# A new order for the first two fifths of a fused attention and gated-convolution kernel

## The chip, the core and the metric

The kernel runs on one core of one Trainium2 chip. A core has five engines that each work through a stream of their own: TensorE (PE in the profile, with its weight loads as PEld), VectorE (DVE), ScalarE (ACT), GpSimd (POOL) and SyncE (SP). They wait for one another through semaphores. Sixteen DMA engines move data between the memory outside the core and its on-chip memory, or within the latter. The metric is the device time of one execution in microseconds (us); lower is better.

## The reference

The inputs are q, k and v of 4 batches, 8 heads, 768 positions and 64 features, a table of sampled blocks, and the weights of a feed-forward stage. First comes block-sparse attention with blocks of 32 positions:

```
scores = scale * q @ k.T
mask   = |block_i - block_j| <= 1, or either block is the first or the last,
         or block_j is one of three sampled for block_i
attn   = softmax(where(mask, scores, -1e9)) @ v
```

The heads of a position are put side by side (512 features) and go through a gated convolution:

```
h    = relu(x @ w_in)                     # 512 -> 1024
conv = sum over k of conv_w[k] * h shifted by k - 1 along the sequence
out  = (h * sigmoid(conv)) @ w_out        # 1024 -> 512
```

## The kernel before, in words

**Tiling.** Two heads of one batch make a pair; there are 16 pairs, numbered P = 0 to 15, four to a batch. The 768 positions are taken in two halves of 384, so the run has eight segments of batch and half (the last is split once more). Scores are computed transposed, 128 keys by 128 queries at a time: eight such blocks fill one 128x1024 buffer `st` of PSUM (the memory that TensorE writes), and this is a unit, u = 0 to 143. A pair takes 4.5 units in each half; pair 0 comes at u = 0 and again at u = 18, pair 4 at u = 36 and u = 54, pair 5 at u = 40.5, pair 8 at u = 72.

**What happens to a unit.** TensorE computes two half units of scores (`s`, line 754) with the keys as weights; 24 more rows of the operands carry the mask, so the mask is added by the same matmul. ScalarE takes the exponential of the whole unit (`exp`, line 765) into a `pt` buffer. TensorE then multiplies by the values with a column of ones beside them (`av`, line 787). There are two `st` buffers, so the scores of a unit wait for the exponential two units back. When a pair is through, VectorE divides by the sums (`rcp`, line 703, and `norm`, line 705).

**Keys and queries.** They are needed transposed. For pairs 0 to 4, TensorE transposes them (`k_tr`, line 476, `q_tr`, line 515) and a copy puts them into the pair's slot (`k_cp`, `q_cp`, line 327, the helper that records all copies). For pairs 5 to 15 the transpose is done in a DMA issued by SyncE, a crossbar turn (`xb`, line 593, one for k and one for q), into a staging buffer, and two copies (`stg_cp`, line 327) put it into the slot. There are five slots. The mask rows of slots 1 and 2 are copied by VectorE; those of slots 3 and 4 by two DMAs of 144 KB on SyncE (`m_dma`, line 368). Pair 4 uses slot 4. Values go through one copy for each pair (`v_cp`, line 327).

**Feed-forward stage.** The normalised result of each pair and half has to be transposed too: with TensorE for the first segment (`x_tr`, line 724), and for later ones with another crossbar turn on SyncE (`x_xb`, line 714, into `xT`). When the four pairs of a segment are there, TensorE multiplies by `w_in` (`f1`, line 906, eight feature groups for a segment, in two entries each), VectorE or ScalarE applies the relu (`relu`, line 928 on VectorE, 926 on ScalarE), VectorE does the convolution (`mul`, line 967, `add`, line 976), ScalarE a tanh (line 1015), VectorE the gate (`g1`, line 1018, `g2`, line 1023). The second product (`f2`, line 833) waits for the gate of the feature groups that it reads; its four entries for an output block take two feature groups each. A copy (`ev`, line 327) and a DMA (`out`, line 841) end it.

**Loads.** GpSimd issues all loads of q, k, v and of the two weight matrices (line 240). Between them stand `pace` entries: a copy of a single element that reads a tile, so that GpSimd waits until that tile has landed (line 668) or until the exponential of a certain unit is done (line 425).

**What sets the order.** Each piece of work is an entry of a list (`op`). An entry has one or two engines that can do it, the buffers it takes, and guessed costs. A planner worked out an order from the costs before the kernel was written down; only its result is in the file, in the string `ORDER`. `put_down` reads it: two characters give the entry's number, a letter the engine where there is a choice (P, A, V, G, S), and a digit for each buffer that the entry takes. The kernel then issues the entries in that order, and every engine works through its own in turn:

```
o = ops[64 * CODE.index(line[x]) + CODE.index(line[x + 1])]
...
    e = ENGINES[line[x]]
...
for b in o.allocs:
    b.index = CODE.index(line[x])
...
    o.fn(e)
```

Semaphores follow from what each entry reads and writes. An engine never goes past an entry that waits: what stands behind it in its stream waits too.

Of the kernel before, what the change touches and what calls it, by code (L numbers as in the profile page):

```python
# [25 lines left out]
53415j5B60Q5k5E11RV35F5o18V5p5t5G71mV5J05K0L5u15C4I15L01nV5O15P4JV05D0H5405H5Q15X055V5Y5v25I0B5M5w5N5Z25R5S601
421M15T3615U5x15+06236505yV665V0435/0R5WV674630I1z16a1441S46b1BVhk01AV6c56f06g451T64hl6h668hn1hmV046220ho6n1hpV
6o6s0ht06p747hI02416t69hJ6dhC16u048hDhL256x1hK6yhEA6e49hu2a1hM6z16C0hq1hvV4ahr2c0hN6DhsVhw04bhx2d6E2hQ16K16L23V4
hz1hR6M34chA2i26P0hT6Q6ihyA6j1hO4d6q2k26U1hBV6R46V1N0hS1U14e2l6r6W5hU6Z06+1OV6/61PV7211VV473hF06k0747hGhY26v7a0
h+7bhV6w6l6A6B6F6GhHV6N06m17c0hW1X06H16Oi437f11ZA6S6ThP02601WA7g7k0hZ6X6Y7l7h1hX70ii127h/717m26I7p17q1YV756J7r3  # L30
i07x0ic0i5761i17y772id782e17C17z4i77d7e7Di27ii67j2f7n7E57o7H0i87I7s7ti37A0i97B7F797M17u37G7vij7J628V07Nik7w29V
7O7ie7Kia7R07Sib2m27L7P7Q2bV02jA17Z17+7T02gV1if2niligV07/18202s4f832q3imV17Uio0842ip7W04g1+02hV87188iqAir17X2t3
is8938c0itV8d2v2u7V1iA08e4iM48k1808liNiBiO8m58p08qiPix1iy8r62rV28u1iQ812w08586iCV8aiR8v8bizV8z08A8w72oV2iu07Y2
iv2pV8f8g8B08n08E1iwV8F2x1/18h18oiS8G18s8M0iU02D2E48NiD0iW8O2iE2A8i2B08t8R120V8SiFA8xiV8W02G8T32F8y8C8D21V8XiJ0
j018Y5j18/190iKiX914970j2988HiY8I18P9968Q8U8J2j39c18ViG1iLViZ9d8Z8K9h09i9e7iTiH8L8+j492939j0i+943i/8jiIAjm09a0
9m19n959r02O9o12P1j82jy196jzj92Lj59sja9z19bjb9f9t29g2H19kjnjc9l9Aj6jd9p2R9q2M2j79u2I9E09F9B39v1jejA2Qjfjo9G49J1
9KjB9L5jp2WjCV22X19C9O0jqA39P9w02yV39W19D9Q69X9xjH1jI9y39Y7jE0jF9/0a0jGA1jJV0E2S2a412Z2+0jK1a10k039Ha5k1jN0a61
jLk22TjOjMVa90aajPAk3ae1302/afab2k84ihjT1jUk49Iag39M0JjQ09N9Rka9Sam0jVA9T29Z00Fan35k53639+a2jR2zVa3ao4ar1asjSV
jZ1j+kg0at5aw0khaxjW0310k9ay6a7jrjX2JV4aB1a8aCkbjYAacadahaD79UaJ0aKkcjg0aL0jh2KVaO1aPaj1j/VjiaQ1k6aT0ko1aUjjak
kdai1apaqkpaY1alaZaV22CV3js12NV4aukjavaza+3aAinaEk71aFb10b2ki32jtjkA4kkb91b34bakrju9VaG3jvkebb52YV038be0392aH  # L40
kC0klaM0kqbfaIaNaRkfaSbg6bj1aWkmbkksaXa/kDjwA02UV03dbo03abl7bp2VVjxb0kw13bknb4ktb51kx3cbw1bq0bxkukykvkEby1b60
33V13jbB0kz37A1bCkAV3bG1bHkFbD2b7kI1kGV1b80kJbI3bcbL034VbMkL0bN4kKVkM3e1bQ1kNVbdbRbhbil42bm3mbS53k0kR13fbY0l5
bZ3n3bnl6kO0b+6c11l7jDc2kSl8c37kP3rkTVbr3obsc60c7bt1kQAbz0bu3pbAcb1c80cclc3bE3qkX1ldbFl9kYlecj0cklfcd1kU0kZVbJ
bKbObPlgbTcl2bU1co1bV2b/lal11bWcplhkVlbbXct0kWAc0c4lic5cq3c9calk4cuk+0ljbvk/cv4lll2celmcy1cfl0A3s2czln3AcD03x
cE3B4cA5cg3cm0l3Vcncrcscwlo3tlG0cF6ls0cL1lA1ltlpcxcMch3FcQ03CcBlvcRcN7cicClH3DlucGcH1cS1lBlwkBcOlqcPcV1lxlrcW
kHc+0c/3gV2cT3icX0lClyjlcUlzlId02d613hVd7cYlJd83lDlKV03G0db0lEA2dc3uV3dg13O3P1dhdd4lY0lZ3y2cZdi5m81l+V0m93EcI0
dl0cJd1dm3Tl/0maV3Qdn6m03vVdq13Rd2drm1Vd90m51ds73L3M1dy0mk1dzm20ml3SdA0m33Hmmm63ZdD1mn3+3dEm7AdadI0m4AmolLdJdF2
mb1d323lV23U1me0d4mfdK1ms2mcdemgVdN1dOmdAdfmtdjdkdP3dodpmA3dV0dWmCdtmh0dX4mBd+1d/du1mDcK1dBdCe05mimEe30d5e4mu
lM1mjAdv1dGe563VmvdHdLe81dwdMe9dQmpmwdRlNmI4dY0ea7dZlS0dS3mqlOmr0mFed0mJeelTmxmKlUdTlPef0mLe1lVmGe2mMel1lWA3em
3zV3e6eq0myen2e7ebmzermW0mHlQA1ecev13IV43KlFdxdUlX3wewmNegmXmQ1es1mOmRmPeh1ex3mS3JVmTei0eA0ejmUA4eBmY3WV0ek2mZ  # L50
# [5 lines left out]
oJgjgFoNgJ1gkoB1ouAoOoCgG1oU1gKgo1oy0oVgpgL3gtoWgugyozoXgR0oDAgSoPgzoAAgZ1gA3gH0oKgT4oa1gBgIgMoQobgO0g+p03oRgC0
h20p1h3gDAgN1ocoSg/5p2odoL1pk0oeA1p3plgPhb1p4pmAgUgQ0pt1oYh46gVh00pupw2o40gW2pvAgXh1pyh5gYo5p5pxo6pzoZo7h71p6
mVpn1p7o8A0poo+hcoTppApq0h8prhd7o/h61pE4pe1pFpsApfpApgpHh90phpU0haAhepVhfpiA2p80hg3hhp9pBpGpjpapXhi1pIpbhjApM3
qf1pcA4pNqgpCqhAqi0pdpOpJqjpPqc1ofqt0qkApDquqdpQqv1nZqy1qzpKqeAql0qwpRpLqmo9qo0qxqpqnApWq01qq2q1qA4qrpYq60qspZ
qD0pSqEq7pTqF1qBqI0p+qGp/q8qHq2qCq3q9q4A2qJqaA4qKq5qLqbqO1qMA1qPqQqRqNSqU0qSA3qVqWqXqTSqYAqZA  # L60
"""


# [1022 lines left out]
```

## Time and profile before

| | |
|---|---|
| median of 3 runs | 206.25 us (206.09 to 206.26) |
| profiled execution | 205.76 us, of which the span of instructions is 204.0 us |
| TensorE busy | 197.6 us (97%), 2408 matmuls |
| ScalarE busy | 190.0 us (93%) |
| VectorE busy | 182.5 us (89%) |
| GpSimd busy | 57.5 us |
| DMA traffic | 25.93 MB, 53341 packets |

The profile gives one execution. A busy time is a sum over instructions and takes in the time from an instruction's start to its end; instructions of one engine overlap by some hundredths of a microsecond, so the distance between the starts of two neighbours (called the pitch below) is what an instruction costs its engine. In the tables of stretches, each engine has its busy time and, in brackets, the number of its instructions; the DMA share is the mean over 16 engines and can come out over 1 since packets overlap. In a timeline, a row is a start, a length, and a merged run of like instructions; SPq and POOLq are the issuing of DMAs, whose data land later.

The median is 0.49 us over the profiled execution; the profiled execution is 1.76 us over its span.

### The profile page before, as it was taken

The page shows a single profiled execution, that of the slowest core. Times are in us where ns is not written, and L with a number is a line of the kernel's source. Part 1 is how long each engine was busy: PE and PEld are TensorE (multiplying, and loading weights), DVE is VectorE, ACT ScalarE, POOL GpSimd, SP SyncE. Part 2 cuts the span into 40 slices and gives each one's busy share as a digit, 9 for nine tenths or more (in the row PEclk, how much of TensorE's full clock was granted, in tenths as well). Part 3 has the DMA queues.
Part 4 walks back from the last instruction along what each step waited for, and adds up shares of the span by engine and source line. Part 5 has one row for each costly group of instructions (what it writes and reads, how often), then busy time and mean ns, then how long its engine had stood idle before and what let it go on. Part 6 is the DMA issues. An engine that isn't in the chain of part 4 may idle for free.

```text
span 204.0 us, 6214 instructions
## 1 busy us (share of the span) xinstructions
PE 197.6 (97%) x2408; PEld 143.3 (70%) x2408; DVE 182.5 (89%) x572; ACT 190.0 (93%) x251; POOL 57.5 (28%) x112
## 2 busy tenths in 40 slices
...
GB/s 137 163 207 204 197 138 133 149 150 137 94 157 106 139 126 184 191 121 130 148 80 172 96 138 239 140 155 170 78 112 23 39 16 64 16 10 59 190 70 206
DMA packets 53341, 25.93 MB, mean 127 GB/s; under 512 B 39352, under 2 KB 50320, under 8 KB 53312
## 3 DMA queue, kind: packets, MB, share of 16 engines
...
HBM read 23.08 MB, written 6.29 MB: 144 GB/s over the span
## 4 chain that ended last, share of the span: by engine, by line
PE 72%; DVE 9%; ACT 8%; DMA 4%; issue 3%; POOL 3%; ACTq 0%
PE st L754 22%; PE mix L833 18%; PE mix L906 16%; PE av L787 13%; ACT pt L765 7%; DMA nat<-in_q_dram 4%; DVE m L967 3%; DVE m L976 2%; DVE hE L928 1%; POOL nat L240 1%; PE mix L818 1%; PE st L833 1%; DVE qk L327 1%; DVE xtok L705 1%; POOL vn L240 1%
## 5 line engine op out<-in xcount | busy, mean ns | idle before, releaser
L765 ACT ACTIVATE pt<-st 128x1024 bf16<-128x1024 f32 x144 | 140.6, 1041 | 2.4 <-PE st L754 2.0
L754 PE MATMUL st<-qk 88*128 88x256 bf16 (+2 forms) x600 | 89.7, 267 | 1.3 <-ACT pt L765 1.1
L787 PEld LDWEIGHTS <-pt 128*128 128x128 bf16 x1152 | 53.7, 97 | 14.0 <-ACT pt L765 0.5
L754 PEld LDWEIGHTS <-qk 88*128 88x128 bf16 x600 | 48.5, 97 | 19.8 <-issue 2.0
L787 PE MATMUL av<-vt,pt 128*128 128x65 bf16 x1152 | 60.0, 193 | 0.1
L906 PE MATMUL mix<-xT,winb 128*128 128x384 bf16 (+2 forms) x288 | 54.0, 307 | 0.1
L967 DVE TENSOR_SCALAR m<-hE,cw 128x382 bf16<-128x382 bf16 (+2 forms) x192 | 49.7, 320 | 0.5 <-ACT hE L926 0.2
L833 PE MATMUL mix<-woutb,gT 128*128 128x512 bf16 x176 | 47.0, 379 | 0.3 <-DVE gT L1023 0.2
L976 DVE TENSOR_TENSOR m<-m 128x764 bf16<-128x764 bf16 (+2 forms) x64 | 33.7, 534 | 0.5
L906 PEld LDWEIGHTS <-winb 128*128 128x128 bf16 x288 | 24.3, 97 | 9.1 <-issue 0.5
L1015 ACT ACTIVATE m<-m 128x764 bf16<-128x764 bf16 (+2 forms) x32 | 26.4, 831 | 0.9 <-DVE m L976 0.8
L833 PEld LDWEIGHTS <-gT 128*128 128x128 bf16 x184 | 15.5, 97 | 10.7 <-DVE gT L1023 0.5
L425 POOL COPY pace<-pt 1x1 bf16<-1x1 bf16 x24 | 6.0, 250 | 53.0 <-ACT pt L765 52.9
L928 DVE TENSOR_SCALAR hE<-mix 128x384 bf16<-128x384 f32 x31 | 16.9, 552 | 3.2 <-PE mix L906 3.0
L705 DVE TENSOR_TENSOR xtok<-av,rcp 128x384 bf16<-128x384 f32 (+2 forms) x36 | 18.3, 507 | 0.4
L1023 DVE TENSOR_TENSOR gT<-m,hE 128x764 bf16<-128x764 bf16 (+3 forms) x36 | 18.1, 512 | 0.5
L240 POOL DMA_DIRECT2D nat<-in_q_dram x23 | 17.4, 758 | 2.5 <-issue 2.3
L926 ACT ACTIVATE hE<-mix 128x384 bf16<-128x384 f32 (+2 forms) x33 | 16.4, 509 | 0.7 <-PE mix L906 0.5
L327 DVE COPY qk<-stg 64x1536 bf16<-64x1536 bf16 x22 | 12.2, 555 | 0.4
L1018 DVE TENSOR_SCALAR m<-m 128x764 bf16<-128x764 bf16 (+3 forms) x36 | 11.8, 335 | 0.7 <-ACT m L1015 0.4
L240 POOL DMA_DIRECT2D vn<-in_v_dram x16 | 11.6, 727 | 2.5 <-issue 1.6
L327 ACT COPY o2s<-mix 128x512 f32<-128x512 f32 (+1 forms) x16 | 8.9, 564 | 3.5 <-PE mix L833 2.5
...
## 6 DMA issues: line engine op xcount, KB each, us to landing
...
vn<-in_v_dram POOLq DMA_DIRECT2D x16, 192.0 KB, 4.6
nat<-in_k_dram POOLq DMA_DIRECT2D x15, 192.0 KB, 4.6
nat<-in_q_dram POOLq DMA_DIRECT2D x7, 192.0 KB, 5.7
...
```

The lines of the kernel that those rows point to most:

```text
L240: return op(name, {eng: occ}, lambda e: on(e).dma_start(out=dst(), in_=src), prio, deps, dma=(kind, service), **kw)
L327: return (nc.scalar.copy if e == "ACT" else nc.vector.tensor_copy)(out=dst, in_=src)
L705: nm = op("norm", {"DVE": t_dps(128 * C)}, lambda e: nc.vector.tensor_tensor(out=xtok_t[xk.index][:, 0:C].rearrange("p c h d -> p h c d"), ...
L754: nc.tensor.matmul(out=st[:, 128 * x:128 * (x + n_)], lhsT=QK_t[s][0:88, 1, hh, kc, :], rhs=QK_t[s][0:88, 0, hh, at:at + n_, :].rearrange( ...
L765: nc.scalar.activation(out=pt_t[ptb.index], in_=st_t[stb.index], func=AF.Exp, bias=0.0, scale=0.125)
L787: nc.tensor.matmul(out=o[:, off:off + 65], lhsT=pt_t[ptb.index][:, 128 * x:128 * x + 128], rhs=V_t[vslot_b[P].index][:, hh, kc, 0:65], sta ...
L833: nc.tensor.matmul(out=acc(), lhsT=gT_t[gb.index][:, ffc, 128 * t:128 * t + 128], rhs=woutb[:, ffc, :], start=(ffc == 0), stop=(ffc == NFF ...
L906: nc.tensor.matmul(out=mix_t[hb.index][:, w1 * y:w1 * y + w1], lhsT=winb[:, fc, 128 * ffc:128 * ffc + 128], rhs=xT_t[xt_buf[n].index][:, f ...
L928: i = nc.vector.tensor_scalar(out=dst, in0=src, scalar1=0.5, scalar2=0.0, op0=ALU.mult, op1=ALU.max)
L967: i = nc.vector.tensor_scalar(out=m_t[cb.index][:, x, y, 0:w], in0=hE_t[heb.index][:, f0 + y, t0 + x:t0 + x + w], scalar1=cw[:, x, f0 + y: ...
L976: nc.vector.tensor_tensor(out=m[:, a_, :, 0:w], in0=m[:, a_, :, 0:w], in1=m[:, b_, :, 0:w], op=ALU.add)
L1015: th = [op("tanh", {"ACT": t_act(2 * w) + 0.04}, lambda e, cb=cb, w=w: nc.scalar.activation(out=m_t[cb.index][:, 0, :, 0:w], in_=m_t[cb.in ...
```

## The change

Only the string `ORDER` differs. The entries are the same 1783; no instruction is added or taken away. Read entry by entry, the streams of the engines are the same as before from some point to the end: the last 507 of 894 entries on TensorE (from `f1` 39, the second entry of the fourth feature group of the third segment, which before starts at 80.48 us), 157 on ScalarE, 270 on VectorE, 58 of 85 on SyncE, and 35 of 108 on GpSimd. In front of that they are arranged anew. Some buffers get other numbers throughout.

```diff
 ORDER = """
-0405000v010x020bq+107060z03q/r01c0r10w0er208r3r4r5r60c090ar7r81dr9ra0gVrbrcrdrerf1a00hArg0drhrirjrkrl0UA10nV1o1
-rmrnro0frp0SArqrr0W01q20oA0y1010irsrt0XA0rurv160rwrxry12ArzrA0VV0TArB1k1rCrDrE11A130rF0jV0mArG1r4h00YV4i15A0Z1
...
+0405000x0w01020b070603rH0q+1q/1c00yr00cr108r2r3r4r40er5091dr6r7r80dr9rarbrc0ard1a0re0gV0hArfrgrhrirj0nVrk0UA11o1
...
 """
```

Decoded, these are the parts that matter for what follows (a number is the entry's place among entries of its name, counted from 0).

| stream | before | after |
|---|---|---|
| SyncE, after the start | m_dma slot 3, m_dma slot 4, x_xb 0, xb 0, xb 1, x_xb 1, xb 2, xb 3, x_xb 2, x_xb 3, xb 4, xb 5 | m_dma slot 3, x_xb 0, m_dma slot 4, xb 0, xb 1, xb 2, xb 3, xb 4, xb 5, x_xb 1, x_xb 2, x_xb 3 |
| SyncE, then | xb 6, x_xb 4, xb 7, x_xb 6, x_xb 5, x_xb 7, xb 8, xb 9, x_xb 8, xb 10, xb 11, out | xb 6, x_xb 4, xb 8, x_xb 6, x_xb 5, x_xb 7, xb 9, xb 7, xb 10, xb 11, x_xb 8, out |
| GpSimd, after the first five loads | second half of q of pairs 0 and 1, then q of 2, v of 2, k of 3, q of 3 | q of 2, v of 2, k of 3, q of 3, then second half of q of pairs 0 and 1 |
| GpSimd, later | v of pair 10 and q of pair 10 before the pace on u = 63 | both behind the pace on u = 63 |
| VectorE, first half of batch 0 | relu 3, relu 2, mul, v_cp of pair 4 | v_cp of pair 4, relu 2, mul |
| VectorE, at the staging copies | norm 7, stg_cp 0, stg_cp 1 | stg_cp 0, g1, two add, rcp, g2, stg_cp 1, norm 7 |
| TensorE, around the first `f1` of the second segment | s 84, s 85, av, f1 16, f1 17, s 86, s 87, f1 18, f1 19 | s 84, s 85, f2, s 86, s 87, f1 16 to 19 |
| TensorE, the 12 dummy matmuls `fill` | between u = 2 and u = 4 | one at the very start, one at the first transposes, ten spread up to u = 11 |

Twenty-eight entries change between VectorE and ScalarE: six `relu` each way; `stg_cp` 5, an `ev`, an `x_cp`, a `q_cp`, two `k_cp` and a `cast_k` from VectorE to ScalarE; a `v_cp`, an `ev`, three `q_cp`, two `k_cp`, `m_h1` and `m_kh` from ScalarE to VectorE. VectorE ends up with two entries more and ScalarE with two fewer.

More of the change, by code (lines that the diff above doesn't have):

```diff
@@ L26 @@
[L26 to L50, printed above, removed]
@@ L56 @@
[L56 to L60, printed above, removed]
+0405000x0w01020b070603rH0q+1q/1c00yr00cr108r2r3r40er5091dr6r7r80dr9rarbrc0ard1a0re0gV0hArfrgrhrirj0nVrk0UA11o1
@@ new lines @@
+rlrm0frnro0SArp0W01q2rq0VArI0i101rrrsrtru1r0Z1rvrw0XV012A11Arx0/Aryrz0+V1C2rArB0YA4h00lV4i0mV1E30TArC0oVrD0jV
+rErF4j00prG0t4m11F1314n1e115V14V4o11601h00z1fV14r04s1k11jV4t24w11iV4x1Q30v0q4y34B01gV4C4D41bV04K11pV14L0M4k14l
+0s4p4M54q4P00N4Q0rrJ1s04R64U11tV20O4V1v14W71xV4Z04+0P1wV4u4v4z1uV4/0rK5614A570k400C1rLrMrNrO581rP5b00D5c0G1G0
+1J15d20I5g15h1HV34ErQrRrS4F05i31KV4N5l04G05m1LV4O4S1IV4T5n44X5q15r1DV21l11RV34Y5s5504H5z05A511nV5915a5B65215e
+5E1535F5f1mV5j5k5G75o0A5p5J05K1705t5L05O119V1y05P0L5u05C5D5415Q118V415H0Q5I5v25X05w5Y5M425N1M15R5S6015T3615U4I0
@@ new lines @@
+434JV055A5Z25x16236500R665yV5V00B1z1674445WV1S46a11AV6bhk01BV6c5hl450H1T6f06ghmV0hn1466h6220ho6n1hpV6ohq06p76s0
+47hI02416tht1hJhu6u048hL6x1256yhK5+15/636z149642a1hrhM6C06D23V44ahvA682c0hsV696K16E26L6dhQ16e4bhz12dhShNhA1N0
+hR6P0hBA4c6Q2i2hT6i1PA6j0hw16M3hU6q6r4dhx2k2hO6v6k16R46whyV6U16V4e6A2lhY26B6F6W56Z06l6GhC14f1OV6m1hDhVhZ6+721
+h+1U06/6hEV730u6N16O6S1VV41X17477a0260hW7b6T1ZV6X6Y1WV7c0707f17gh/hF07h1hG6H06I717k0277lhP0hHA757607dhX7m27e7p1
+7q1YV2e17iii0i437r37ji07n2f7o7x0i57yi1ic17722m2i6id7z4787C17D28V0ij2n7E5i27H07Ii77s7t7A17J6i87M16J7B7F7u37Ni3
@@ new lines @@
+7Gi97K29Vie797O77L7v7R07Sikia7T0ib7w7Z17+2gV1il7/12bV08202s2q3imV083if8422t3871igV188io04g8931+0ip2hVir1iqVis
+2v2u8c0itV8d8k18l2oV22pAix08m4iM47Piu1iN7Q7U7V02w0iv8e5iPiyiwV8p18qizAiO8u02A8r62B08081iU08viA1iViB8w785iQ8z1
+868a7W18AiXiR8b8f8giCV8E08F8B08h0iJ0iS2jV1iD1iTiK8G18M12DiW2E48NiE8iiLA8R0iFV8O28n08o8SiY8s8t8xj018y8T38C8W12G
+2Fj18X1/08D8Y521V8/08H2rV2iG18J2iH7XiZ9020V8I17Y28P914iIV8Q97198j28U8V8Z996j32H19c09di+jm0i/9e79h19ij48+jn9j0
+j829m0ja929njy1j58K2O932P19r1j98L9a09o19b9f943j69s9gjb9k9ljz9t28jjc9p9z0j79q9Ajd9E195jo9B39F96je9ujAjf9v19G49C
@@ new lines @@
+9J02I9Kjp9L6jBjqV29O12x9PjCA39w19W09x9X9Q79DjE00E2S2jF9Y0jH1jGV1jI9/1a0jJAjK02Z2yV32La11a402M1a5k03jN12+0jLk1
+a639HjOk22Ra912QjMVaajPAae0k3afab52W30jT02X2k84jU9Ik4ag29M2/jQ10J9N9R9Sam1kajVA9Z0an35k53639T29+0Fa2jRa3ao42zV
+ar0as2TjZ0jSVj+at6aw1kg0axjW1kh9y3ay7a7jXk9aB02JV4a8aCjYAacihkbadahaD0aJ19UaKjg1kcaL1jh2KVaO0aPjiaj0j/VaQ3aT1
+310aUk6jrjjko1kdai1akapaqaY0kpaZaV5aljs02CV3au2NV4avaza+2kjaAaEaFinb11k71b2jtjkA4ki32b90b34bakkjukrjv9Vbb6aG3
+ke38be1392kC12YV0aHklaM0bfkqaNaIaRaSbg7bj0kfaWbkkmaXa/kDksjwA13dbo12UV03abl0bpjxb0kw02VV3bb4ktb51knkx3cbw0bq1
@@ new lines @@
+bxkukykvkEby3b6133V13jbB1kz37A1bCkAV2bG0bHkFbD5b7kI0kGV0b80kJbI2bcbL134VbMkL1bN4kKVkM3e1bQ0kNVbdbRbhbil42bm3m
+bS63k0kR03fbY1l5bZ3n4bnl6kO1b+7c10l7jDc2kSl8c30kP3rkTVbr3obsc61c7bt0kQAbz0bu3pbAcb0c81cclc3bE3qkX0ldbFl9kYlecj1
+cklfcd3kU1kZVbJbKbObPlgbTcl5bU1co0bV2b/lal10bWcplhkVlbbXct1kWAc0c4lic5cq2c9calk4cuk+1ljbvk/cv4lll2celmcy0cfl0A
+3s2czln3AcD13xcE3B3cA6cg3cm0l3Vcncrcscwlo3tlG1cF7ls0cL0lA0ltlpcxcMch3FcQ13CcBlvcRcN0cicClH3DlucGcH1cS3lBlwkBcO
+lqcPcV0lxlrcWkHc+1c/3gV2cT3icX1lClyjlcUlzlId05d603hVd7cYlJd82lDlKV1db1lEA3dc3uV3dg03O3P1dhdd4lY1lZ3G03y1cZdi6
@@ new lines @@
+m80l+V0m93EcI1dl1cJd1dm3Tl/1maV3Qdn7m03vVdq03Rd2drm1Vd90m50ds03L3M2dy1mk1dzm21ml3SdA1m3mmm63ZdD0mn3+3dEm7AdadI1
+m4AmodJdF5mb0d323lV2me1d4mfdK3ms2mc3HdemgVdN0dOmdAdfmtdjdkdP2lLdodpmA3dV1dWmC3U1dtmh1dX4mBd+0d/du1mDdBdCe06mi
+mEe31e4mulM0mjAdv0dGe57mvdHdLe80dwdMe9cK1dQmpmwdRlNmI4d5dY0ea0dZlS1dS3mqlO3Vmr0mFed1mJeelTmxmKlUdTlPef1mLe1lV
+mGe2mMel0lWA2em3zV3e6eq1myen5e7ebmzermW1mHlQA0ecev03IV43KlFdxdUewlXmNegmX3wmQ0es3mOmRmPeh1ex2mS3JVmTei1eA1ejmUA4
+eBmY3WV0ek2mZeI0m+V1eJn90lRna3XVn613Yn73NV43/A0eC4eK6m/eN1nbVn8AeOeS0eTeP7nw0n30nyn4n01eU0nxn1n5VeX1eYn2Anzeo
```

17 lines of the change are left out of this document (9 added, 8 removed).

## The prediction

> **What bounds the kernel now.** I read the page's shares and its chain first, then a table of stretches, then the timelines of the engines around the places that the new order touches.
>
> ```profile
> span 204.0 us, 6214 instructions
> PE 197.6 (97%) x2408; PEld 143.3 (70%) x2408; DVE 182.5 (89%) x572; ACT 190.0 (93%) x251; POOL 57.5 (28%) x112
> PE 72%; DVE 9%; ACT 8%; DMA 4%; issue 3%; POOL 3%; ACTq 0%
> ```
>
> ```profile
> 5.00:36.00 31.00, 30.22 (x418) 24.06 (x418) 27.14 (x85) 29.76 (x38) 18.71 (x36) 1.00 1.20 173
> 36.00:46.00 10.00, 9.04 (x131) 6.97 (x128) 9.89 (x32) 9.95 (x14) 3.39 (x7) 1.00 1.21 150
> 46.00:62.00 16.00, 16.00 (x212) 11.66 (x210) 15.08 (x41) 16.00 (x20) 4.32 (x10) 1.00 0.86 123
> 62.00:76.00 14.00, 13.68 (x171) 9.29 (x170) 12.75 (x38) 13.58 (x18) 5.40 (x12) 1.00 1.01 131
> 76.00:80.50 4.50, 4.50 (x45) 3.09 (x43) 3.79 (x13) 4.50 (x7) 1.82 (x3) 1.00 1.33 197
> 80.50:180.00 99.50, 99.50 (x1217) 70.53 (x1216) 93.82 (x282) 97.29 (x124) 19.82 (x36) 1.00 0.65 110
> ```
>
> TensorE's clock is 1.00 in every stretch. From 80.5 to 180 us TensorE has no idle time, and its stream there is the same before and after; so the change can act only through the moment at which TensorE reaches that point, which I call the handover: `f1` 39 at 80.48 us, inside this run:
>
> ```profile
> 74.25 0.56 DVE L1023 TENSOR_TENSOR gT<-m,hE 128x772 bf16<-128x772 bf16 x1
> 75.22 1.03 PE L833 MATMUL mix<-woutb,gT 128*128 128x512 bf16 x4
> 79.83 1.14 PE L906 MATMUL mix<-xT,winb 128*128 128x384 bf16 x6
> ```
>
> The work in front of the handover is the same matmuls. Only idle time can go or come: 0.78 us from 5 to 36, 0.96 from 36 to 46, 0.32 from 62 to 76, and 1.10 in the first 5 us. So no order gains more than about 3 us, and one that keeps the startup gains at most 2. In that front part ScalarE and VectorE are nearly full too (9.95 and 9.89 of 10 from 36 to 46): a stall of either comes out on TensorE.
>
> Nothing there waits for the crossbar. The staging tile's own view has one wait of 0.2 us:
>
> ```profile
> L593 SPq DMA_TRANSPOSE stg<-nat x22: 1209/1238/2119, 42.0 to 136.0; - x22
> PEld L754: 0.2, 1
> DMA to landing us min/median/max: 2.8/4.7/7.7
> ```
>
> **The change part by part.** I follow the new streams with pitches from this trace and note when the three engines pass four places.
>
> *Up to 33 us: the loads.* The second halves of q for pairs 0 and 1 go behind four loads, and so q of pair 2, for which TensorE stands 0.17 us at 14.26, leaves at 5.2 instead of 6.6.
>
> ```profile
> 6.60 0.77 POOL L240 DMA_DIRECT2D nat<-in_q_dram  x1
> 14.26 0.40 PE L515 MATMUL mix<-ident,nat 128*128 128x128 bf16 x4 [0.17 <-DMA nat<-in_q_dram]
> POOL pace L668 <- DMA woutb<-in_moe_w_out_dram: 3.5, 2, 2.3
> 28.72 0.71 POOL L240 DMA_DIRECT2D vn<-in_v_dram  x1
> vn<-in_v_dram POOLq DMA_DIRECT2D x1, 192.0 KB, 4.3
> 33.58 0.56 DVE L928 TENSOR_SCALAR hE<-mix 128x384 bf16<-128x384 f32 x1 [0.33 <-PE mix L906]
> 34.66 0.35 DVE L327 COPY vt<-vn 128x768 bf16<-128x768 bf16 x1
> ```
>
> That, the spread dummies and copies moved off ScalarE let the exponentials run up to 1.5 us earlier by u = 26. It is worth little, because of the next entry: VectorE now copies the values of pair 4 ahead of `relu` 2. They leave at 28.72 and need 4.3, so they are there at 33.0, and GpSimd's chain up to there hangs on the landing of weight loads (3.5 us of waits) that stay where they are. VectorE arrives at about 31.5 and stands; behind it wait `relu` 2, its PSUM buffer `mix`, and so the next transpose on TensorE. It goes on at 33.1, and `relu` 2 starts at 33.4: before, 33.58. The early gain is given back but for 0.2, and 0.27 of copying is done.
>
> *33 to 47.5 us: the first crossbar turns.*
>
> ```profile
> 40.09 0.54 DVE L705 TENSOR_TENSOR xtok<-av,rcp 128x384 bf16<-128x384 f32 x1
> 39.16 0.71 POOL L240 DMA_DIRECT2D nat<-in_k_dram  x1 [0.21 <-issue]
> 7.51 1.79 SPq L368 DMA_DIRECT2D qk<-qk  x2
> 40.65 1.28 SPq L714 DMA_TRANSPOSE xT<-xtok  x1
> 42.04 2.69 SPq L593 DMA_TRANSPOSE stg<-nat  x2
> xT<-xtok SPq DMA_TRANSPOSE x1, 5.3
> 45.00:47.00 2.00, 2.00 (x25) 1.33 (x24) 1.97 (x8) 2.00 (x3) 0.00 (x0) 1.00 1.27 219
> 47.00:47.50 0.50, 0.50 (x19) 0.50 (x18) 0.47 (x3) 0.50 (x2) 0.00 (x0) 1.00 0.23 38
> ```
>
> `norm` 4, ten VectorE pitches behind `relu` 2 (some 4.6 us), ends near 37.9 instead of 40.6, so SyncE starts 2.7 us sooner. But between its first turn and the next now stands the mask copy of slot 4, 144 KB, which before went out with its sister within 1.79 us from 7.51. It needs SyncE for half of that, 0.9, and the DMA engines at their busiest. The turn that went out at 40.65, behind loads still on their way, landed only after 5.3 us, when these were through; the DMA share is over 1 until 47 and 0.23 after it, so the turns issued by 44.8 were done then. The new burst holds the same loads and turns up to `xb` 1, plus the copy: at 219 GB/s its 144 KB are 0.67 us. Beside short rows such a copy takes partly idle bandwidth; bounds are 0 and 0.67, and I take the middle: `xb` 1 lands at 47.5 (47.1 to 47.8). VectorE comes to its first staging copy, 13.2 us of pitches behind the value copy, at 46.2: it stands 1.3 us. The mask itself is wanted by the scores of pair 4 at about 44.6. Issued at 39.3, between two loads, it should be there by 44.1; behind the load of 40.14 it would take till 46. TensorE has 1.3 us to spare before the next place, so even that costs at most 0.4.
>
> *47.5 us to `f1` 16.*
>
> ```profile
> 48.58 0.56 DVE L705 TENSOR_TENSOR xtok<-av,rcp 128x384 bf16<-128x384 f32 x1
> 49.06 1.13 DVE L327 COPY qk<-stg 64x1536 bf16<-64x1536 bf16 x2
> 49.68 2.51 SPq L714 DMA_TRANSPOSE xT<-xtok  x2
> 50.49 0.60 PE L754 MATMUL st<-qk 88*128 88x128 bf16 x4
> 53.16 0.81 PE L906 MATMUL mix<-xT,winb 128*128 128x384 bf16 x4
> L714 SPq DMA_TRANSPOSE xT<-xtok x29: 1107/1205/1721, 40.7 to 182.9; - x29
> DMA to landing us min/median/max: 2.3/2.7/5.3
> ```
>
> Between the two staging copies stand now `g1`, two `add`, `rcp` and `g2`; the second ends 2.9 us behind the first's start, at 50.5, about as before (50.2). The scores of pair 5, which stood at 50.71 (second half of the unit at 50.49), stand at 50.6. From there TensorE has 2.8 us up to `f1` 16, and 0.15 of waiting for the gate: 53.55. `norm` 7 ends at 51.0; the last turn that `f1` 16 needs leaves at 51.1 and at the shortest landing of its tile, 2.3 us, is there at 53.4. SyncE, with nine turns at 1.27 and the copy from 37.9, is free by 50.2. So `f1` 16 starts at F = 53.6, 0.44 later than before, with 0.07 more of TensorE's work done.
>
> *From `f1` 16 to the handover.*
>
> ```profile
> 55.10 0.56 DVE L928 TENSOR_SCALAR hE<-mix 128x384 bf16<-128x384 f32 x1 [0.16 <-PE mix L906]
> 55.58 0.55 DVE L967 TENSOR_SCALAR m<-hE,cw 128x386 bf16<-128x386 bf16 x2
> ```
>
> VectorE sets the pace here. Before, it enters at 55.10, 1.94 behind `f1` 16, and ends `g2` 7 at 74.81: F + 21.65. After, the two feature groups stand side by side and VectorE takes the first relu itself, at F + 0.9. Up to `g2` 7 it gains work: three relu at 0.47, a value copy (0.27), `norm` 8 with its `rcp` (0.57), less two relu and a staging copy (0.58), 0.73 in all. Its entries sum to 19.6 us of pitches; with 0.3 of waits `g2` 7 ends at F + 20.8. Two pairs of `f2` follow, and 4.3 us of TensorE's work: handover at F + 26.6 against F + 27.32. ScalarE comes out alike: the exponential of u = 64 at F + 25.3 against F + 26.0. The cover that hides the staging copy moved to ScalarE (1.3 us) is TensorE's wait for F. The last turn of segment 2, 2.3 us behind `norm` 11 (F + 20), precedes its `f1` (F + 23.3) by 1.
>
> *Behind the handover.* Values and q of pair 10 leave some 6 us later, and SyncE stands at the turn that needs them until about 87. Pair 10 comes at u = 81, some ten units later: 0, and 0.5 if the outputs queued behind it come late.
>
> **The sum.** +0.44 to `f1` 16, -0.72 from there: -0.28. The profiled execution takes 205.76, so 205.48; the median of the runs is 0.49 higher: 205.97, and I say 206.0.
>
> **Rivals.** *Faster: the turns do not wait behind the loads.* If `xb` 1 landed before VectorE comes at 46.2, VectorE and TensorE alone would set `f1` 16: F = 52.8. Then -0.36 - 0.72 = -1.1, 205.2. For it: the view of the tiles has turns of 2.3 to 5.3 us, so many went through quickly; against it, the turn of 40.65 and the share of 1.27.
>
> The Trainium skill, page "DMA: Bandwidth & Descriptors", section "Queues, rings and completion order", states that each DMA engine goes round robin between the queues that have work, a packet at a time. By that rule a turn would share the engines with the loads instead of landing behind them, and the sum would be this rival's. This trace has the turn of 40.65 at 5.3 us, against 2.3 for the quickest, which is on the other side.
>
> ```profile
> 53.18 0.70 POOL L240 DMA_DIRECT2D vn<-in_v_dram  x1
> ```
>
> *Slower: the last turn meets a load.* The value load of pair 7 waits for the exponential of u = 40, which now comes 0.4 sooner: the load leaves near 52.5. If the turn before `f1` 16 left behind it, it would land after up to 5.3 instead of 2.3. The margin is 1.4 us of SyncE being late (it needed 2.1 instead of 1.24 for one turn). Half the price is +1.5: 207.5. *Slower: the hand-overs between 33 and 45.* There, ScalarE, VectorE and TensorE follow each other with some 0.1 us to spare at ten places; if the 0.96 us of idle time come a second time, 206.0 + 0.9 = 206.9. *The change does nothing that matters*, since no engine waited for the crossbar: 206.25, inside my forecast.
>
> **How the numbers follow.** Within 0.2% (0.41 us, about what a measurement of this kernel can tell from no change): 0.35, the forecast. Faster: 0.28, the first rival and parts of it. Slower: 0.37, of which 0.12 the load and 0.25 the hand-overs and what I can't see. The range goes from 205.2, the first rival, to 207.5, the second. The forecast's own range is 205.85 to 206.65.
>
> **What would show it.** VectorE idle for a microsecond ahead of the value copy near 32 and again ahead of the first staging copy near 46.5; the mask copy landing before 44.5; `f1` 16 between 53.4 and 54; handover 26.6 behind it. The forecast is wrong if `f1` 16 comes before 53 or behind 54.5, if the scores of pair 4 wait for the mask, or if TensorE shows idle time behind 80 us.

## The result, and the profile after

The changed kernel takes 213.83 us (median of four runs, 211.51 to 215.09), the kernel before, on the same chip, 206.17 us (205.87 to 206.26): a ratio of 1.0337, with a 95% interval of 1.0249 to 1.0425. The prediction was 206.0, with a range up to 207.5. It was wrong by more than 7 us. The profiled execution took 214.35 us; its span is 212.6, which is 8.6 more than before.

The page of the changed kernel: span, busy times, the granted TensorE clock in 40 slices (of 5.3 us each), and the shares of the chain.

```profile
span 212.6 us, 6190 instructions
PE 199.4 (94%) x2390; PEld 143.3 (67%) x2408; DVE 182.1 (86%) x574; ACT 190.8 (90%) x249; POOL 58.2 (27%) x112
PEclk9999999999958999999999999999999999999999
PE 74%; DMA 10%; issue 5%; DVE 5%; ACT 3%; POOL 0%; SPq 0%; DVEq 0%; POOLq 0%
```

The work is the same. DMA has gone from 4% of the chain to 10%, and the clock, which was full in every stretch before, has two slices at 5 and 8 tenths. The table of stretches shows where (columns as in the prediction; the second fence is a finer cut around the low clock):

```profile
46.00:62.00 16.00, 11.62 (x102) 7.10 (x103) 10.24 (x26) 11.21 (x12) 3.58 (x7) 0.90 1.01 143
62.00:76.00 14.00, 14.00 (x176) 10.16 (x175) 11.74 (x39) 11.74 (x15) 2.77 (x6) 0.87 0.36 43
88.80:188.00 99.20, 98.61 (x1207) 70.22 (x1217) 93.35 (x280) 96.85 (x124) 23.47 (x41) 1.00 0.74 116
```

```profile
55.90:59.50 3.60, 0.32 (x1) 0.10 (x1) 0.22 (x1) 2.04 (x2) 1.80 (x4) 0.91 1.23 162
59.50:64.90 5.40, 5.38 (x32) 3.28 (x32) 3.16 (x8) 1.81 (x2) 0.00 (x0) 0.50 0.50 74
64.90:66.00 1.10, 1.10 (x10) 0.63 (x8) 0.17 (x1) 0.12 (x1) 0.57 (x2) 0.64 0.00 0
```

TensorE stands 4.4 of the 16 us from 46 to 62. From 59.5 on it works without a gap, but at half its clock, until 65.7. Behind the handover it is full again (ten matmul records are missing there). So everything was lost ahead of the handover, as the prediction had it; the size was not foreseen. TensorE's waits between 30 and 66 us, and the chain's three transfers that hold it up:

```profile
PE mix L906 <- DMA xT<-xtok: 3.6, 2, 3.3
PE mix L515 <- DVE hE L928: 1.1, 2, 0.8
PE st L754 <- DMA qk<-qk: 0.7, 1, 0.7
```

```profile
29.79 4.32 DMA vn<-in_v_dram
41.28 5.90 DMA qk<-qk
54.78 4.70 DMA xT<-xtok
```

The first transfer is the value load of pair 4, the second the mask copy of slot 4, the third the last crossbar turn of segment 1. The timelines show the third: GpSimd's value load of pair 7, SyncE's three turns of segment 1 (1.3 apart, so the last is the one of 54.78), and TensorE's second `f1` entry.

```profile
54.31 0.70 POOL L240 DMA_DIRECT2D vn<-in_v_dram  x1 [0.28 <-issue]
52.18 3.81 SPq L714 DMA_TRANSPOSE xT<-xtok  x3
55.92 0.32 PE L906 MATMUL mix<-xT,winb 128*128 128x384 bf16 x1 [0.30 <-DMA xT<-xtok]
59.52 0.80 PE L906 MATMUL mix<-xT,winb 128*128 128x384 bf16 x2 [3.28 <-DMA xT<-xtok]
```

The load goes out 0.47 us ahead of the turn. The turn then lands after 4.70 us, and TensorE stands 3.28 us for it.

The row of the handover, `f1` 39, in the changed kernel:

```profile
88.82 0.49 PE L906 MATMUL mix<-xT,winb 128*128 128x384 bf16 x2
```

The same places in the profiles of both kernels, in us:

| place | before | after | difference |
|---|---|---|---|
| `relu` 2 starts (VectorE) | 33.58 | 34.41 | +0.83 |
| first turn leaves (SyncE) | 40.65 | 39.94 | -0.71 |
| first scores of pair 4 (u = 36) start | 44.87 | 47.22 | +2.35 |
| last turn of segment 1 leaves | 50.98 | 54.78 | +3.80 |
| value load of pair 7 leaves | 53.18 | 54.31 | +1.13 |
| F: `f1` 16 starts | 53.16 | 55.12 | +1.96 |
| handover: `f1` 39 starts | 80.48 | 88.82 | +8.34 |

Behind F: 0.30 + 3.28 us of standing; half a clock for 5.40 us and 0.36 of one for 1.10, that is 2.7 + 0.4 = 3.1; with F's 1.96 together 8.6. Of that 0.3 comes back: the 0.32 us that TensorE stood between 62 and 76 before are gone. That is the 8.34 at the handover.

The runs of the kernels with such a stand differ by up to 5.7 us among themselves; in the four of this one the mean clock over the span falls as the time grows (0.992 at 211.51 and 213.32 us, 0.984 at 214.35, 0.982 at 215.09).

### The profile page after: what moved, and what is told of

Its sections match the earlier page's. It is cut to its first block, busy times and chain, and to the rows that moved or that the text cites. A ratio compares the mean times of both kernels' runs of the same rounds, so it can differ in the third digit from the quotient of the medians.

```text
span 212.6 us, 6190 instructions
## 1 busy us (share of the span) xinstructions
PE 199.4 (94%) x2390; PEld 143.3 (67%) x2408; DVE 182.1 (86%) x574; ACT 190.8 (90%) x249; POOL 58.2 (27%) x112
## 4 chain that ended last, share of the span: by engine, by line
PE 74%; DMA 10%; issue 5%; DVE 5%; ACT 3%; POOL 0%; SPq 0%; DVEq 0%; POOLq 0%
PE st L754 24%; PE mix L906 18%; PE mix L833 17%; PE av L787 13%; DMA qk<-qk 3%; ACT pt L765 3%; DMA xT<-xtok 2%; DMA vn<-in_v_dram 2%; DMA woutb<-in_moe_w_out_dram 2%; DVE m L967 2%; DMA sbi<-in_sampled_blocks_dram 1%; DVE qk L327 1%; PE mix L818 1%; PE st L833 1%; PE av L987 1%
## 5 line engine op out<-in xcount | busy, mean ns | idle before, releaser
L754 PE MATMUL st<-qk 88*128 88x256 bf16 (+2 forms) x600 | 90.7, 270 | 2.5 <-DVE qk L327 0.9
L906 PE MATMUL mix<-xT,winb 128*128 128x384 bf16 (+2 forms) x288 | 55.8, 315 | 4.2 <-DMA xT<-xtok 3.6
L787 PE MATMUL av<-vt,pt 128*128 128x65 bf16 x1152 | 59.3, 194 | 0.3
L967 DVE TENSOR_SCALAR m<-hE,cw 128x382 bf16<-128x382 bf16 (+2 forms) x192 | 49.2, 316 | 0.3
L833 PE MATMUL mix<-woutb,gT 128*128 128x512 bf16 x158 | 44.2, 379 | 0.7
L976 DVE TENSOR_TENSOR m<-m 128x764 bf16<-128x764 bf16 (+2 forms) x64 | 33.7, 534 | 0.6
L425 POOL COPY pace<-pt 1x1 bf16<-1x1 bf16 x24 | 7.2, 300 | 60.0 <-ACT pt L765 51.2
```

Of the source, the lines that this page charges most:

```text
L754: nc.tensor.matmul(out=st[:, 128 * x:128 * (x + n_)], lhsT=QK_t[s][0:88, 1, hh, kc, :], rhs=QK_t[s][0:88, 0, hh, at:at + n_, :].rearrange( ...
L787: nc.tensor.matmul(out=o[:, off:off + 65], lhsT=pt_t[ptb.index][:, 128 * x:128 * x + 128], rhs=V_t[vslot_b[P].index][:, hh, kc, 0:65], sta ...
L833: nc.tensor.matmul(out=acc(), lhsT=gT_t[gb.index][:, ffc, 128 * t:128 * t + 128], rhs=woutb[:, ffc, :], start=(ffc == 0), stop=(ffc == NFF ...
L906: nc.tensor.matmul(out=mix_t[hb.index][:, w1 * y:w1 * y + w1], lhsT=winb[:, fc, 128 * ffc:128 * ffc + 128], rhs=xT_t[xt_buf[n].index][:, f ...
L967: i = nc.vector.tensor_scalar(out=m_t[cb.index][:, x, y, 0:w], in0=hE_t[heb.index][:, f0 + y, t0 + x:t0 + x + w], scalar1=cw[:, x, f0 + y: ...
L976: nc.vector.tensor_tensor(out=m[:, a_, :, 0:w], in0=m[:, a_, :, 0:w], in1=m[:, b_, :, 0:w], op=ALU.add)
```

## The experiments

In the diffs, a line is an entry in the stream of the engine named; everything else in ORDER is as in the kernel given. The kernel before was run beside each, at 205.99, 206.24, 206.10 and 206.07 us in the four groups, in the order in which the kernels stand in their labels (1 to 4, 5 to 8, 9 to 11, 12). Entries have their numbers from the section on the change: `xb` 4 and 5 and `stg_cp` 4 and 5 belong to pair 7, and `ld_k` 7 loads the keys of pair 8; the expectations name the pair one too low in these places.

### The last turn and the load

Theory: the stand comes from the turn going out behind the load, and the clock falls because of the stand. First the changed kernel with only the load put off:

```diff
 GpSimd, changed kernel
 pace (u = 40)
-ld_v 7, ld_k 7, pace, ld_nq 0
 pace (u = 42)
+ld_v 7, ld_k 7, pace, ld_nq 0
```

> The changed kernel with nothing altered but GpSimd: the loads of values and k of pair 7 (and the small q load) leave behind the next pacing copy, some 1.5 us later, so behind the last turn of segment 1. Theory (that turn is late because it meets the load): the turn still leaves at 54.8 but lands within 2.6 us, near 57.3 instead of 59.5; TensorE's stall ahead of the second f1 falls from 3.3 to about 1.2 us, the granted clock stays at 1.00, and the time falls by 2.2 for the wait and some 2.8 for the clock: 208 to 209.5. If the stall alone counts and the clock falls anyway: 211.5. Rival (the turn is slow by itself): no change, 212 to 215.

209.37 us, ratio 1.017 (1.011 to 1.022). The turn left at 54.60, nearly as before, and landed after 2.30 us. TensorE's rows at the second `f1`, and the table of two stretches:

```profile
56.95 0.97 PE L906 MATMUL mix<-xT,winb 128*128 128x384 bf16 x5 [0.93 <-DMA xT<-xtok]
55.00:60.00 5.00, 3.74 (x39) 2.41 (x37) 3.42 (x9) 3.80 (x5) 3.46 (x6) 1.00 0.73 104
60.00:66.00 6.00, 6.00 (x69) 4.12 (x68) 5.96 (x20) 5.91 (x8) 1.59 (x4) 1.00 1.15 115
```

A stand of 0.93 instead of 3.28 and a clock of 1.00: the loss against the kernel before falls from 7.7 to 3.4 us, so 4.3 us are this one meeting. The rest is F, which came at 54.87, 1.71 later than before, and the two short stands of 0.34 and 0.93; the handover came at 83.66, 3.18 later than before. Then the opposite, the same defect built into the kernel before, once with the load in its place and once with the load put off too:

```diff
 SyncE, kernel before
 x_xb 2
-x_xb 3
 xb 4, xb 5
+x_xb 3
```

```diff
 GpSimd, kernel before, in addition in the second of the two
-ld_v 7, pace, ld_nq 0, ld_k 7
 pace (u = 42)
+ld_v 7, pace, ld_nq 0, ld_k 7
```

> The kernel before with one entry moved: the last turn of segment 1 goes behind the two staging turns of pair 6, so it leaves near 53.6, behind the value load of 53.2. Theory (a late turn meets the load, and the long stand halves the clock): it lands near 58.3, TensorE stands 4 us ahead of its f1 and then shows a granted clock of 0.5 for 5 to 6 us; 4.0 + 2.7, less some slack: 211 to 213. Rival (the stand alone, no clock): 209 to 210. Rival (hidden): 206 to 207.

> As the run with the last turn late in the kernel before, and GpSimd's loads of pair 7 behind the next pacing copy too, near 55. Theory: the turn, at 53.6, is ahead of the load again, lands near 55.9, TensorE stands 1.5 to 2 us, the clock stays at 1.00: 207 to 208.5. Rival (it is the place of the turn in SyncE's queue that counts, not the load): 211 to 213.

213.11 us (ratio 1.028, 1.020 to 1.036) and 207.86 us (1.011, 1.006 to 1.016), as the theory had it (the first 0.1 over its range). TensorE's row at the stand and the stretches around it, first with the load in its place, then with the load put off:

```profile
58.99 0.48 PE L906 MATMUL mix<-xT,winb 128*128 128x384 bf16 x1 [4.89 <-DMA xT<-xtok]
54.00:58.90 4.90, 0.11 (x1) 0.00 (x0) 1.17 (x3) 0.62 (x1) 2.93 (x6) 0.78 1.13 142
58.90:63.30 4.40, 4.31 (x20) 2.41 (x20) 1.66 (x7) 2.27 (x3) 0.00 (x0) 0.50 0.86 132
63.30:66.00 2.70, 2.70 (x36) 1.98 (x34) 2.43 (x7) 2.11 (x4) 0.00 (x0) 0.95 0.39 73
```

```profile
55.66 0.32 PE L906 MATMUL mix<-xT,winb 128*128 128x384 bf16 x1 [1.48 <-DMA xT<-xtok]
55.70:62.00 6.30, 6.30 (x72) 4.54 (x72) 4.86 (x14) 5.91 (x7) 2.58 (x5) 1.00 0.89 110
```

The turn left at 54.25 and 53.31 and took 4.70 and 2.30 us. The place of one `pace` entry on GpSimd's stream decides over 5 us. The sum holds here too: 4.89 of standing and 4.40 x 0.50 + 2.70 x 0.05 = 2.3 of clock are 7.2, and the handover is 7.33 later than in the profile before.

The turns put back in the order of before, in the changed kernel:

```diff
 SyncE, changed kernel
 xb 0, xb 1
+x_xb 1
 xb 2, xb 3
-xb 4, xb 5, x_xb 1
 x_xb 2, x_xb 3
+xb 4, xb 5
```

> The changed kernel with SyncE's turns of segment 1 and pair 5, 6 in the order of before (x 1 behind xb 1, x 2 and 3 ahead of xb 4 and 5); the mask copy stays late. Theory (late last turn): the last turn of segment 1 leaves at 52 to 52.5, ahead of the value load of 54.3, and lands within 2.6 us; TensorE waits under 1 us there, the granted clock stays at 1.00 from 55 to 70, and the time is 206.5 to 208.5. Rival (the mask copy is the root): 212 or more. Rival (the clock falls by itself): granted clock again near 0.5 for some 5 us.

213.98 us (1.037, 1.034 to 1.041): no better, against my expectation. The time alone is what both rivals gave; the trace shows another cause. The last turn of segment 1 did leave at 52.16 and landed in 2.28. But now `xb` 5 goes out at 54.76, behind the load of 54.26, and lands after 5.28 us, and the entry that wants it at once is `stg_cp` 5, which the change has given to ScalarE. ScalarE's and TensorE's rows, and the stretch behind:

```profile
60.12 1.47 ACT L327 COPY qk<-stg 64x1536 bf16<-64x1536 bf16 x1 [3.70 <-DMA stg<-nat]
62.56 1.49 PE L754 MATMUL st<-qk 88*128 88x128 bf16 x6 [3.36 <-ACT pt L765]
62.50:67.50 5.00, 4.94 (x36) 3.29 (x36) 3.36 (x11) 4.07 (x6) 0.88 (x2) 0.50 0.32 43
```

ScalarE stands, its exponentials stand behind the copy, TensorE stands for them, and the clock falls again. In the kernel before `xb` 5 also took 4.66 us, but its copy stood on VectorE at 59.80, when the turn had landed. So it is not one turn: any turn near that load can be late, and what counts is how soon it is wanted.

Nor is going out first enough. The profiles of all fourteen kernels have these turns around the value load of pair 7 (the shortest landing is 2.3 us for a turn into `xT` and 2.8 for one into staging):

| turn leaves | turns | lands after |
|---|---|---|
| 0.83 to 2.58 us ahead of the load | 22 | 2.28 to 2.79 us |
| 0.45 to 0.68 us ahead of it | 4, all into staging | 3.87 to 4.44 us |
| 0.07 to 0.88 us behind it | 11 | 4.56 to 6.16 us |

A turn had to lead the load by some 0.8 us. The last turn of the changed kernel, 0.47 behind, was 1.3 us too late for that, by this estimate from the table.

### What made the turn late

F was 1.96 later than before. The suspects are the mask copy and the value copy of pair 4. The mask copy alone, moved in the kernel before:

```diff
 SyncE, kernel before
 m_dma slot 3
-m_dma slot 4
 x_xb 0
+m_dma slot 4
```

> The kernel before with one entry moved: the mask copy of slot 4 behind the first turn, as the change has it. Theory: the copy lands 5 to 6 us after it is issued at 42, near 47.5; the scores of pair 4, due at 44.87, wait 2 to 2.6 us, part of which later slack takes up; SyncE is 1.1 us later, and the last turn of segment 1, at 52, still goes ahead of the value load: 207 to 208.5, clock 1.00 there. Rival (the copy is hidden, as the prediction had it): 206.0 to 206.6.

207.17 us (1.0045, 1.002 to 1.007): the low end of what the theory gave. The interval reaches into the rival's range too, but the trace shows the wait. TensorE's row at the scores of pair 4:

```profile
46.05 0.39 PE L754 MATMUL st<-qk 88*128 88x384 bf16 x2 [0.83 <-DMA qk<-qk]
```

The copy, out at 42.66, landed after 3.35 us; it is not hidden, but it is a small part. Each suspect put back in the changed kernel alone:

```diff
 SyncE, changed kernel
 m_dma slot 3
+m_dma slot 4
 x_xb 0
-m_dma slot 4
```

```diff
 VectorE, changed kernel
-v_cp 4
 relu 2, mul 3
+v_cp 4
```

> The changed kernel with one entry put back: the mask copy of slot 4 goes out right behind its sister, before the first turn, as before. Theory (late last turn): the scores of pair 4 no longer wait (0.74 us), SyncE saves 1.1 us ahead of the last turn of segment 1, which then leaves near 53.6 instead of 54.78; the value load of pair 7 also leaves earlier (exponential of u = 40 less 0.7), near 53.5, so the race between the two is close: either the turn still lands after more than 4 us and the time is 211 to 213, or it goes ahead and the time is 206.5 to 208. Rival (the mask copy is the root of it): time at or below 206.5, and no stall over 1 us ahead of the second f1 of segment 1.

> The changed kernel with VectorE's copy of the values of pair 4 put back behind relu 2 and the product after it. Theory (the stall at 34 us is VectorE waiting for that landing): VectorE's wait of 1.7 us is gone or moves behind relu 2, the transposes of q at 34 to 35 on TensorE no longer stand 0.75, f1 16 starts 0.3 to 0.9 earlier; but the last turn and the load of pair 7 both come earlier and meet again: 211 to 213.5. Rival (that stall is the root of the late turn): below 209.

212.67 us (1.023, 1.017 to 1.029) and 213.6 us (four runs from 209.16 to 214.81, so no interval is given). Neither removes the meeting of turn and load: the turn leaves 0.07 and 0.46 us behind the load. Nor does either move F: 55.05 and 55.33. With the mask early the value copy still holds VectorE, for 2.2 us in that profile, and the scores of pair 4 start at 47.15 without any wait; with the value copy back, `relu` 2 starts at 32.35, but TensorE then stands 1.3 us for the mask:

```profile
PE st L754 <- DMA qk<-qk: 1.3, 1, 1.3
```

The two stand side by side. Both put back, with the load put off as well so that no meeting clouds it:

> The changed kernel with the mask copy early, the value copy of pair 4 behind relu 2 and the loads of pair 7 behind the next pacing copy; the turns stay in the changed order. Theory (the two early delays hide each other, so each alone gave nothing, and both together set f1 16): f1 16 starts near 54.0 instead of 55.1, TensorE then stands 1 to 1.5 us for the last turn, which SyncE sends near 53.5; 207.5 to 208.7, against 209.4 with the loads alone. Rival (other things set f1 16): 209 to 209.6.

208.47 us (1.011, 1.007 to 1.015), against 209.37 with the load alone. The intervals of these two overlap; one profile of each shows the step: F at 53.63 instead of 54.87, and the turn at 52.82 instead of 54.60. A stand of 0.89 us stays, since six staging turns still go ahead of the last turn.

### The two halves of the change by themselves

The startup: the changed order up to the exponential of u = 22 (near 30 us), then the order of before.

> The changed order up to the exponential of u = 22 (near 30 us), the order of before from there on: what the changed startup (loads of k and values ahead of the second halves of q, copies off ScalarE) is worth by itself. Theory: TensorE is 0.7 us behind at 17 us, but has that back by 30 us because its work was only put off; the value load of pair 4, which GpSimd sends 1 us later, is now copied behind relu 2 and hurts nobody: 206.0 to 206.6. Rival (the 0.7 stays): 206.7 to 207.2. Rival (the early exponentials are worth what they run ahead by, up to 1.5 us): 205.0 to 205.8.

206.37 us, ratio 1.0002 (0.998 to 1.003): nothing. The exponential of u = 26 started at 34.13, against 34.16 before: the early gain does not outlast the change back.

The other half: the order of before up to `f1` 16, then the changed order, first with only `stg_cp` 5 moved to VectorE, then with `stg_cp` 4 and 5 both later:

```diff
 VectorE, first of the two: order of before up to f1 16, then the changed one
 relu 9, stg_cp 4, mul 12, mul 13, add 8, relu 10, mul 14, mul 15, mul 16, add 9
+stg_cp 5
 rcp 8, add 10
```

```diff
 VectorE, second of the two
 relu 9
-stg_cp 4
 mul 12, mul 13, add 8, relu 10, mul 14, mul 15, mul 16, add 9, rcp 8, add 10
+stg_cp 4, stg_cp 5
```

> The order of before up to f1 16 (53.16 us), from there the changed order, with one exception: the staging copy that the change gives to ScalarE stays on VectorE, five entries behind. This leaves the early part and its late turn out and shows what the changed order of the second half of the front is worth. By the prediction's step (f1 16 to the handover in 26.6 instead of 27.3): 205.3 to 205.7. If the changed order there is worth nothing by itself: 206.0 to 206.5. If new waits come up there: over 206.7.

> As the kernel with the order of before up to f1 16 and the changed order behind it, with both staging copies of pair 6 on VectorE behind add 10, some 4 us later than the change has them, where the turns they need have landed. By the prediction's step (f1 16 to the handover in 26.6 instead of 27.3 us): 205.3 to 205.7. If the changed order there gains nothing by itself: 206.0 to 206.6. In both cases no stand over 1 us and a clock of 1.00; if the stand of the earlier hybrid (3.0 us on VectorE's relu) was not these copies: 210 to 211.5.

211.27 us (1.024, 1.022 to 1.027) and 207.44 us (1.006, 1.004 to 1.008). In the first I had overlooked that `stg_cp` 4 needs both turns of its pair, so VectorE stood for `xb` 5 (issued 0.22 us behind the load) in ScalarE's place:

```profile
59.95 0.55 DVE L327 COPY qk<-stg 64x1536 bf16<-64x1536 bf16 x1 [3.62 <-DMA stg<-nat]
62.55 1.44 PE L906 MATMUL mix<-xT,winb 128*128 128x384 bf16 x4 [3.01 <-DVE hE L928]
62.50:65.50 3.00, 2.95 (x24) 1.99 (x24) 2.94 (x10) 0.85 (x1) 0.00 (x0) 0.50 0.57 50
```

The second has no such stand, and is slower than before all the same, above both ranges that I had given. From F to the handover it takes 81.80 - 54.12 = 27.7 us, of which 0.5 is a wait for the copies that I had put late.

Last, the changed kernel with four places put back or moved: the mask copy, the value copy and the turns as in the diffs above, and both staging copies as here (`stg_cp` 5 leaves ScalarE for it):

```diff
 VectorE, changed kernel, beside the three diffs above
 relu 9
-stg_cp 4
 mul 12, mul 13, add 8, relu 10, mul 14, mul 15, mul 16, add 9, rcp 8, add 10
+stg_cp 4, stg_cp 5
```

> The changed kernel with four places put back: the mask copy early, the value copy of pair 4 behind relu 2, the turns in the order of before, and the two staging copies of pair 6 on VectorE behind add 10. Theory (everything that was lost is these places and the clock that falls with them): the startup keeps 0.75 us of its loss, f1 16 starts at 53.7 to 54.3, its last turn leaves ahead of the load of pair 7, the clock stays at 1.00: 206.0 to 207.2. If the rest of the change costs by itself: 207.5 or more.

207.88 us (1.008, 1.005 to 1.011), above my range. F came at 54.02, as expected, and the clock was 1.00; 0.7 us of waiting for the late staging copies is again my own doing. F to the handover took 28.0; what VectorE has to do with that stands under step 4 below. No version tried is faster than the kernel before.

## Why the prediction was wrong

**The rival that I gave 0.12 is what happened, at nearly three times its price.** "The last turn meets a load" was named, with the right load, the right turn and the right mechanism (up to 5.3 instead of 2.3 us). Three things were wrong with its numbers. I took half the price, 1.5, and the meeting cost 4.3. I took the margin of 1.4 from a load at 52.5 and a turn at 51.1; they left at 54.31 and 54.78, and a lead of some 0.8 was needed, so that no more than 0.6 was ever to spare. And I did not carry the stand on to the clock: every stretch that I had read showed 1.00, and so I treated the clock as given. The clock cost 3.1 us, nearly as much as the stand.

For eight of the kernels, the longest stand of TensorE between F and the handover and the time at half clock, in us:

| kernel | longest stand | clock 0.50 from, to | for |
|---|---|---|---|
| changed, load later | 0.93 | none | |
| before, turn and load late | 1.48 | none | |
| before, then changed order | 3.01 | 62.34, 65.75 | 3.41 |
| changed, value copy back | 3.20 | 60.77, 64.18 | 3.41 |
| changed | 3.28 | 58.87, 65.70 | 6.83 |
| changed, turns as before | 3.36 | 61.57, 68.40 | 6.83 |
| changed, mask early | 3.51 | 57.77, 64.59 | 6.82 |
| before, turn late | 4.89 | 56.77, 63.59 | 6.82 |

These times lie on a grid: in each trace the clock goes up for the first time in the first 8 us, and from there every fall and rise is a whole number of steps of 3.41 us away (in the changed kernel 16 steps from 4.26 to the fall and 2 more to the rise). The steps of the changed kernel around the fall:

```profile
55.46:58.87 3.41, 0.48 (x2) 0.10 (x1) 0.63 (x2) 2.48 (x3) 2.25 (x5) 1.00 1.08 139
58.87:62.28 3.41, 2.76 (x11) 1.46 (x11) 1.49 (x3) 0.00 (x0) 0.00 (x0) 0.50 1.06 148
62.28:65.70 3.42, 3.42 (x27) 2.29 (x26) 1.67 (x6) 1.94 (x2) 0.27 (x2) 0.50 0.02 4
65.70:69.11 3.41, 3.41 (x53) 2.65 (x52) 3.28 (x11) 2.91 (x4) 0.60 (x1) 1.00 0.47 62
```

In the six steps that ended in a fall TensorE had worked 0.48 to 1.36 us; in every other step at full clock up to its last matmul, in all fourteen profiles, 2.16 or more. The half clock ended behind a step with 3.20 or more of work and went on behind one with 2.76 or less. So a stand costs clock by where it lies on the grid, and not by its length alone; and only the part of the half clock behind the stand costs time. That the runs of one kernel differ fits this: 3.41 us at half clock take 0.008 off the mean over the span. Of the four runs of "before, turn late" one took 210.08 us with a mean clock of 1.000, the others 213.08 to 213.90 with 0.982 or 0.983. Of the six of "before, turn and load late" two took 209.45 and 210.36 us with 0.989 and 0.991, the others 207.53 to 207.88 with 0.998 or more; their traces were not kept, so how long TensorE stood in these two is not known.

The Trainium skill, page "TensorE: Matmul & The Clock Gate", section "Part 1: The HAM clock gate (the "warmup" mystery)", states that a gate watches TensorE in free-running windows of about 3.4 us, halves the clock behind an idle window and gives it back after a busy one. The traces agree in the half clock and in the grid of 3.41 us; but the window need not be idle throughout, since up to 1.36 us of work in it did not hold the clock, and a stand of 3.01 us, shorter than the page's window, was enough here. This was the rule that spoke against the change, and the prediction did not weigh it.

**Step 1, up to 33 us.** Right that VectorE would stand for the values of pair 4 and give the early gain back; mis-sized. I had the load leave at 28.72, as before, because its chain hung on weight loads. It hangs one link further back on the second-half load of q that GpSimd issues when TensorE has freed its buffer. Rows of GpSimd before and after, and VectorE's after:

```profile
20.51 0.71 POOL L240 DMA_DIRECT2D nq<-in_q_dram  x1 [5.11 <-PE mix L515]
```

```profile
23.27 0.72 POOL L240 DMA_DIRECT2D nq<-in_q_dram  x1 [7.81 <-issue]
34.13 0.36 DVE L327 COPY vt<-vn 128x768 bf16<-128x768 bf16 x1 [1.70 <-DMA vn<-in_v_dram]
```

In both kernels the load goes out 0.54 us behind the end of that transpose on TensorE, which the change has put 2.76 later. The value load left at 29.79, landed at 34.11 instead of 33.0, and `relu` 2 started at 34.41 instead of 33.4.

**Step 2, 33 to 47.5.** `norm` 4 ended at 39.91 (forecast 37.9): one us from step 1, the rest hand-overs. With that the mask copy left at 41.28, behind the loads and not between them, and landed at 47.17; I had 44.1, with 46 as the bad case, and TensorE's 0.74 us stand was the cost I had bounded at 0.4. `xb` 1 landed at 48.5, 0.7 behind the end of my bounds.

**Step 3, to `f1` 16.** This is the step that failed. I had SyncE "free by 50.2", at nine turns of 1.27 us from 37.9. It began at 39.94, and the six staging turns took 1.61 each, with the gaps between them:

```profile
42.43 9.66 SPq L593 DMA_TRANSPOSE stg<-nat  x6
```

The trace of before had such rows (3.46 for two), and I took the quick ones:

```profile
46.12 3.46 SPq L593 DMA_TRANSPOSE stg<-nat  x2
```

So SyncE, not `norm` 7 (ended at 52.18), set the last turn. It left 3.7 us behind the forecast: SyncE began 2.0 later and took 2.5 more than forecast for what stood ahead, some 2 of them on the six staging turns, and 0.9 had been spare between 50.2 and 51.1. That put the last turn behind the load, and with it came 3.6 us of standing and 3.1 of clock, for which the forecast had nothing: 6.7 of the 8.34 at the handover.

**Step 4, `f1` 16 to the handover.** Forecast 26.6. Without the stands and the lost clock the changed kernel takes 33.7 - 3.6 - 3.1 = 27.0; with three places put back 28.3 - 0.9 = 27.4; behind the order of before 27.7, with 0.5 of waiting for the late copies in it. Before it is 27.3. The gain of 0.72 was to come from VectorE's taking the first relu at F + 0.9. It did, at F + 0.86 behind the order of before and at F + 0.96 with four places put back or moved, and it worked from there to the end of `g2` 7 without a wait that the profile shows. But that took 21.1 and 21.35 us, of which 0.5 is a staging copy that the change does not have there; my sum of the entries was 19.6. So `g2` 7 ended at F + 22.0 and F + 22.3, not at F + 20.8. The sum was about 1 us short, more than the gain. And the cover that I named for the staging copy on ScalarE, "TensorE's wait for F", holds only while its turn is early: with the turns as before, the copy stood 3.7 us.

**Step 5, behind the handover.** Right: 8.34 us at the handover, 8.6 at the end.

**The other rivals.** The faster one is out: turns behind loads landed after 4.70 us in the changed kernel and in the kernel before with the turn late, turns that led them by 0.83 us or more after 2.28 to 2.79. By the round-robin rule of the Trainium skill (page "DMA: Bandwidth & Descriptors", section "Queues, rings and completion order") it would have been the outcome; the last turn of the changed kernel landed at 59.5, between the value load issued 0.47 us before it (58.3) and the k load issued 0.22 us behind it (60.1), in the order of issue. The runs don't show whether that order comes from the queues or from something behind them. "The change does nothing that matters" holds for the startup alone (ratio 1.0002).
